# Issuing a kernel's first work ahead of its block, and waiting for its stores behind the block's closing barrier

## The chip, the cores and the metric

The kernel runs on one core of a Trainium2 chip. The metric is the device time of one execution in microseconds. The profile also gives the span, from the first to the last instruction that it recorded in this program. Here the metric is longer than the span (129.3 against 127.56 us in the profiled run of the kernel before). A semaphore is a counter by which the engines and the loads and stores tell each other that something is done; a load or store lands when its last packet is counted on its semaphore. A run is called slow when it lies over 1.5% above the fastest of its kernel.

## The reference

Six cross layers are applied to 4096 rows of 416 numbers in bfloat16:

```python
def reference(x0, ws, bs):          # (4096, 416), (6, 416, 416), (6, 416)
    x = x0
    for l in range(ws.shape[0]):
        x = x0 * (x @ ws[l] + bs[l]) + x
    return x
```

## The kernel before

The rows are worked through in four stages of 1024, the features as three blocks of 128 and a tail of 32. TensorE multiplies, VectorE and ScalarE add the bias and multiply by x0, GpSimd does the tail. All the code of the engines stands in one block: each engine jumps into its own body at the block's start (my reading of the program; the traces have no record of this jump) and out of it at its end (the trace before records SyncE's branch alone, at 127.177 us), and the end of the block is a barrier of all five (in the same trace GpSimd collects the others at 127.379 and releases them at 127.456). The change touches only the two edges of the block.

```python
    with ExitStack() as es:
        block = es.enter_context(nc.Block())
        # ... buffers, semaphores ...

        @block.sync
        def _(sp):
            # ...
            sp.dma_start(bsa_sb[1:L + 1, :], bs[:, :]).then_inc(s_bs, 16)
            sp.dma_start(xin_sb[:, 0:2, :], x0_v[:, 0:2, :]).then_inc(s_xin[0], 16)
            sp.dma_start(xin_sb[:, 4:6, :], x0_v[:, 4:6, :]).then_inc(s_xin[2], 16)
            sp.dma_start_transpose(x0T_sb[:, :, 768:SB], x0[768:SB, 0:DF]).then_inc(s_x0T[0], 16)
            # ... weights, stages ...
            store(sp, 0, 2, 0)
            store(sp, 4, 2, 2)
            sp.wait_ge(s_out, 16 * (NS + 3))

        @block.tensor
        def _(pe):
            # ...
            fill(10)          # 40 matmuls of constants, to keep TensorE busy
            bias_sums()       # waits for the biases, the memsets and GpSimd's setup
            fill(1)
            # ... transposes of the first rows; then stages, each layer ~84 matmuls
            # before the first layer's third block of features:
                                pe.wait_ge(s_xin[2], 16)
                                pe.wait_ge(s_xtl0, 16)
                                tail_inputs()

        @block.scalar
        def _(act):
            act.dma_start(xin_sb[:, 2:4, :], x0_v[:, 2:4, :]).then_inc(s_xin[1], 16)
            act.dma_start(w_sb[:, 0, :, :], wmain(0)).then_inc(s_w[0], 16)
            act.dma_start(xtl_sb[:, :, :], x0_v[:, 6:JS, DF:D]).then_inc(s_xtl0, 16)
            # ...
            act.wait_ge(s_o, JS - 2)
            act.dma_start(out_w[:, (j0 + 6) // 2, :, :], o_sb[:, j0 + 6:j0 + JS, :]).then_inc(s_out, 16)
```

## Time and profile before

| | before |
|---|---|
| time, first three runs | 129.58 us median (129.36 to 129.74) |
| span of the profiled run (its time) | 127.56 us (129.3 us) |
| dense part of TensorE | 6.77 to 124.57 us |
| landing of the last store | 127.160 us |

The stretches of the kernel before, cut at the start and the end of the dense part, one row each: length, then busy microseconds and instructions of TensorE, its weight loads, VectorE, ScalarE and GpSimd, then the granted TensorE clock, the DMA share and GB/s.

```profile
0.00:6.77 6.77, 5.58 (x96) 3.64 (x97) 2.12 (x7) 1.94 (x3) 4.34 (x13) 1.00 0.82 202
6.77:124.57 117.80, 117.78 (x2242) 58.45 (x2242) 97.18 (x146) 65.63 (x143) 19.77 (x31) 1.00 0.48 98
124.57:127.60 3.03, 0.00 (x0) 0.00 (x0) 0.59 (x1) 0.00 (x0) 0.00 (x0) 0.99 0.51 191
```

In the middle row TensorE is busy for all but 0.02 us. Nothing that the change touches lies there. The first row is an opening under loads (DMA share 0.82), the last row has one VectorE instruction in it and otherwise stores and barriers.

### The profile page before, as it was taken

What the parts mean: (1) busy time and instruction counts of PE and PEld (TensorE: products, weight loads), DVE (VectorE), ACT (ScalarE), POOL (GpSimd) and SP (SyncE); (2) the same over time, 40 slices, a digit from 0 to 9 for tenths busy, and PEclk for the clock granted to TensorE, in tenths of its full rate; (3) what the DMA queues carried; (4) which work ended last, traced back from release to release, by engine and by line L of the source; (5) the groups of instructions that cost most, each with busy time, mean ns of one, the idle gap of its engine ahead of it and who ended that gap; (6) DMA issues with size and microseconds to landing.
All of it is one profiled execution on the core that took longest, in us unless ns stands there. A gap on an engine that the chain in (4) does not pass through costs nothing.

```text
span 127.6 us, 5176 instructions
## 1 busy us (share of the span) xinstructions
PE 123.4 (97%) x2338; PEld 62.1 (49%) x2338; DVE 99.9 (78%) x154; ACT 67.6 (53%) x146; POOL 24.1 (19%) x44
## 2 busy tenths in 40 slices
PE   7999999999999999999999999999999999999990
PEld 5554545445444445445445445445445444444660
DVE  2349779779779779779789788798797797797872
ACT  0637357377726456475735554574753573576630
POOL 7512202202102013012022023022022022020460
PEclk9999999999999999999999999999999999999999
DMA  3973399400009899710008679950007910620015
GB/s 100 292 182 100 91 214 212 128 0 0 5 8 143 127 117 231 244 47 5 0 5 152 124 121 242 347 161 0 5 0 48 208 22 0 208 64 5 0 63 204
DMA packets 32576, 13.48 MB, mean 106 GB/s; under 512 B 24870, under 2 KB 32556, under 8 KB 32556
## 3 DMA queue, kind: packets, MB, share of 16 engines
q1 hardware_dynamic: 31036, 12.12, 45.7%
q10 hardware_dynamic: 1328, 0.99, 2.5%
q8 instruction: 18, 0.29, 1.0%
q0 software_dynamic: 192, 0.06, 0.2%
q14 instruction: 2, 0.02, 0.1%
HBM read 3.86 MB, written 3.41 MB: 57 GB/s over the span
## 4 chain that ended last, share of the span: by engine, by line
PE 92%; DMA 4%; ACTq 1%; DVE 0%; issue 0%
PE ps L243 78%; PE ps L374 10%; DMA xtl_sb<-in_x_dram 4%; PE ps L422 3%; PE ps L430 1%; DVE o_sb L518 0%; ACTq L526 0%; PE ps L454 0%; ACTq L525 0%; PE ps L390 0%; PE ps L460 0%
## 5 line engine op out<-in xcount | busy, mean ns | idle before, releaser
L505 DVE SCALAR_TENSOR_TENSOR xT_sb<-ps,cb_sb,x0T_sb 128x512 bf16<-128x512 f32 x120 | 81.0, 744 | 16.5 <-PE ps L374 16.4
L243 PE MATMUL ps<-xT_sb,w_sb 128*32 128x512 bf16 (+1 forms) x1596 | 84.2, 364 | 0.0
L243 PEld LDWEIGHTS ps<-xT_sb,w_sb 128*32 128x32 bf16 x1596 | 40.9, 97 | 37.2 <-issue 4.0
L537 ACT ACTIVATE xt_sb<-xt_sb 32x256 bf16<-32x256 bf16 x76 | 31.5, 414 | 15.8 <-POOL xt_sb L220 15.1
L566 ACT ACTIVATE t_sb<-ps,cb_sb 64x256 f32<-64x256 f32 x46 | 21.6, 469 | 31.2 <-PE ps L243 30.9
L220 POOL TENSOR_TENSOR xt_sb<-t_sb,x0t_sb 128x256 bf16<-128x256 f32 x20 | 13.5, 674 | 81.5 <-ACT t_sb L566 81.5
L243 PE MATMUL ps<-x0T_sb,w_sb 128*32 128x512 bf16 (+1 forms) x336 | 18.5, 364 | 0.2 <-DVE x0T_sb L480 0.2
L505 DVE SCALAR_TENSOR_TENSOR xo_sb<-ps,cb_sb,x0T_sb 128x512 bf16<-128x512 f32 x18 | 12.1, 743 | 2.5 <-PE ps L374 2.5
L243 PEld LDWEIGHTS ps<-x0T_sb,w_sb 128*32 128x32 bf16 x336 | 8.6, 97 | 7.7 <-issue 0.8
L374 PE MATMUL ps<-xt_sb,wt_sb 32*128 32x512 bf16 x76 | 11.5, 379 | 0.0
L585 ACT ACTIVATE x0t_sb<-x_sb 32x512 bf16<-32x512 bf16 x12 | 7.5, 626 | 0.3
L390 PE MATMUL ps<-xt_sb,wt_sb 32*128 32x512 bf16 x38 | 7.4, 385 | 0.0
L374 PE MATMUL ps<-xt_sb,wc_sb 32*128 32x256 bf16 x76 | 7.3, 268 | 0.0
L374 PEld LDWEIGHTS ps<-xt_sb,wt_sb 32*128 32x128 bf16 x76 | 2.2, 92 | 8.1 <-DVE xT_sb L505 8.1
L422 PE MATMUL ps<-w_sb,xT_sb 128*128 128x416 bf16 x24 | 5.4, 340 | 0.0
L374 PEld LDWEIGHTS ps<-xt_sb,wc_sb 32*128 32x128 bf16 x76 | 3.8, 93 | 2.2
L220 POOL TENSOR_TENSOR xot_sb<-t_sb,x0t_sb 128x256 bf16<-128x256 f32 x3 | 2.0, 676 | 12.6 <-ACT t_sb L566 12.6
L518 DVE SCALAR_TENSOR_TENSOR o_sb<-ps,x0n_sb 128x416 bf16<-128x416 f32 x6 | 3.3, 586 | 1.1 <-PE ps L460 1.0
L541 ACT ACTIVATE xo_sb<-ps,cq_sb 128x512 bf16<-128x512 f32 x5 | 3.3, 686 | 1.1 <-PE ps L374 1.1
L243 PE MATMUL ps<-const-bfloat16-1.0 128*32 128x256 bf16 x44 | 2.7, 415 | 0.8 <-PEq L612 0.8
L532 ACT ACT_TABLE_LOAD x1 | 1.3, 1283 | 3.6 <-issue 3.6
L422 PEld LDWEIGHTS ps<-w_sb,xT_sb 128*128 128x128 bf16 x24 | 2.0, 98 | 1.4 <-DVE xT_sb L505 0.4
(46 smaller groups left out, 36.8 us busy)
## 6 DMA issues: line engine op xcount, KB each, us to landing
out_dram<-o_sb SPq DMA_DIRECT2D x3, 832.0 KB, 5.7
w_sb<-in_ws_dram SPq DMA_DIRECT2D x5, 312.0 KB, 4.5
x0n_sb<-in_x_dram SPq DMA_DIRECT2D x1, 832.0 KB, 5.5
xin_sb<-in_x_dram SPq DMA_DIRECT2D x2, 208.0 KB, 3.7
out_dram<-o_sb SPq DMA_DIRECT2D x2, 208.0 KB, 2.0
out_dram<-o_sb ACTq DMA_DIRECT2D x2, 208.0 KB, 2.0
w_sb<-in_ws_dram ACTq DMA_DIRECT2D x1, 312.0 KB, 3.7
xin_sb<-in_x_dram ACTq DMA_DIRECT2D x1, 208.0 KB, 2.7
```

The lines of the kernel that those rows point to most:

```text
L220: pool.tensor_tensor(out=dst, in0=t32_sb[:, n % 2, :], in1=x0t_sb[:, s, 0:G], op=ALU.mult).then_inc(s_xt, 1)
L243: return pe.matmul(dst, lhsT=lhsT, rhs=rhs, start=start, stop=True, skip_group_check=True, tile_position=(0, 32 * q),)
L374: return pe.matmul(dst, lhsT=lhsT, rhs=srct[lane(g), cols], start=l == 0 and start, stop=True, skip_group_check=True, tile_position=(32 * ...
L390: pe.matmul(ps[:, NC * h + 2, :], lhsT=wt_sb[lane(g), l, 0:128], rhs=srct[lane(g), :].rearrange("p (b r) -> p b r", b=2)[:, ::-1, :], star ...
L422: pe.matmul(ps[:, NAT_BANKS[t], 0:D], lhsT=xT_sb[:, (L - 1) % 2, k, rows], rhs=w_sb[:, L - 1, k, :], start=t < 4 and k == 0, stop=True, sk ...
L505: dve.scalar_tensor_tensor(out=dst, in0=ps[:, NC * half + c, :], scalar=cb_sb[:, c, l:l + 1], in1=x0T_sb[:, c, o:o + H], op0=ALU.add, op1= ...
L518: dve.scalar_tensor_tensor(out=o_sb[:, j0 + t, :], in0=ps[:, NAT_BANKS[t], 0:D], scalar=1.0, in1=x0n_sb[:, t, :], op0=ALU.add, op1=ALU.mul ...
L532: act.activation(out=x0T_sb[:, 1, h * 256:(h + 1) * 256], in_=psT[:, IN_BANKS[h][1], 0:256], func=ACTF.Copy).then_inc(s_inA, 1)
L537: ins = act.activation(out=buf[lane(g), G:2 * G], in_=buf[lane(g ^ 1), 0:G], func=ACTF.Copy)
L541: act.activation(out=xo_sb[:, NS - 1, c, half * H:(half + 1) * H], in_=ps[:, NC * half + c, :], func=ACTF.Identity, bias=cq_sb[:, c:c + 1] ...
L566: ins = act.activation(out=t32_sb[HALVES[h], n % 2, :], in_=tail(h), func=ACTF.Identity, bias=cb_sb[HALVES[h], NC, l:l + 1],)
L585: ins = act.activation(out=x0t_sb[lane(g), s + 1, :].rearrange("p (b n) -> p b n", b=2), in_=src[:, ::-1, :] if g % 2 else src, func=ACTF. ...
```

## The change

The intent was to take the jump into the block off the path of the first loads, and the closing barrier off the path of the last store. The diff, cut to its core:

```diff
     with ExitStack() as es:
-        block = es.enter_context(nc.Block())
 # ... buffers, semaphores ...
+        for q in range(4 * 10):
+            nc.tensor.matmul(
+                ps[lane(q % 4), 7, 0:256], lhsT=CONST[:, 0:32], rhs=CONST, start=True, stop=True,
+                skip_group_check=True, tile_position=(0, 32 * (q % 4)),
+            )
+        nc.sync.dma_start(bsa_sb[1:L + 1, :], bs[:, :]).then_inc(s_bs, 16)
+        nc.sync.dma_start(xin_sb[:, 0:2, :], x0_v[:, 0:2, :]).then_inc(s_xin[0], 16)
+        nc.sync.dma_start(xin_sb[:, 4:6, :], x0_v[:, 4:6, :]).then_inc(s_xin[2], 16)
+        nc.scalar.dma_start(xin_sb[:, 2:4, :], x0_v[:, 2:4, :]).then_inc(s_xin[1], 16)
+        nc.scalar.dma_start(w_sb[:, 0, :, :], wmain(0)).then_inc(s_w[0], 16)
+        nc.scalar.dma_start(xtl_sb[:, :, :], x0_v[:, 6:JS, DF:D]).then_inc(s_xtl0, 16)
+        nc.gpsimd.memset(ones_sb[:, :], 1.0).then_inc(s_ones, 1)
+        nc.vector.memset(wc_sb[:, :, :], 0.0).then_inc(s_zero, 1)
+        nc.vector.memset(bsa_sb[0:1, :], 1.0).then_inc(s_zero, 1)
+
+        es2 = ExitStack()
+        block = es2.enter_context(nc.Block())
 # ... the same lines leave the bodies of the engines ...
             store(sp, 4, 2, 2)
-            sp.wait_ge(s_out, 16 * (NS + 3))
 # ... end of the last body ...
+        es2.close()
+        nc.sync.wait_ge(s_out, 16 * (NS + 3))
```

More of the change, by code (lines that the diff above doesn't have):

```diff
@@ L111, in tail @@
             return ps[HALVES[h], 6 + h, 0:G]
+        CONST = nc.const_aps.tensor_like(1.0, ones_sb[:, :])
         j0 = (NS - 1) * JS
@@ L138, in load_rows @@
                 ).then_inc(s_x0T[s], 16)
-            sp.dma_start(bsa_sb[1:L + 1, :], bs[:, :]).then_inc(s_bs, 16)
-            sp.dma_start(xin_sb[:, 0:2, :], x0_v[:, 0:2, :]).then_inc(s_xin[0], 16)
-            sp.dma_start(xin_sb[:, 4:6, :], x0_v[:, 4:6, :]).then_inc(s_xin[2], 16)
             sp.dma_start_transpose(x0T_sb[:, :, 768:SB], x0[768:SB, 0:DF]).then_inc(s_x0T[0], 16)
@@ L176, in _ @@
             store(sp, 4, 2, 2)
-            sp.wait_ge(s_out, 16 * (NS + 3))
         @block.gpsimd
         def _(pool):
-            pool.memset(ones_sb[:, :], 1.0).then_inc(s_ones, 1)
             def load_wc(i, g):
@@ L246, in tile_mm @@
                 )
-            const = nc.const_aps.tensor_like(1.0, ones_sb[:, :])
             def fill(n):
@@ L252, in fill @@
                     for q in range(4):
-                        tile_mm(ps[lane(q), 7, 0:256], const[:, 0:32], const, q, True)
+                        tile_mm(ps[lane(q), 7, 0:256], CONST[:, 0:32], CONST, q, True)
             def tail_inputs():
@@ L283, in bias_sums @@
                 ins.then_inc(s_cbp, 1)
-            fill(10)
             bias_sums()
@@ L470, in _ @@
         def _(dve):
-            dve.memset(wc_sb[:, :, :], 0.0).then_inc(s_zero, 1)
-            dve.memset(bsa_sb[0:1, :], 1.0).then_inc(s_zero, 1)
             dve.wait_ge(s_cbp, 1)
@@ L524, in _ @@
         def _(act):
-            act.dma_start(xin_sb[:, 2:4, :], x0_v[:, 2:4, :]).then_inc(s_xin[1], 16)
-            act.dma_start(w_sb[:, 0, :, :], wmain(0)).then_inc(s_w[0], 16)
-            act.dma_start(xtl_sb[:, :, :], x0_v[:, 6:JS, DF:D]).then_inc(s_xtl0, 16)
             for g in (1, 3):
```

## The prediction

Two names in it, and in the expectations further on, stand for one thing in the traces: the serpentine, or the runtime's barrier, is the row of nine raises of semaphore 2 behind the kernel, from 127.799 to 128.345 us in the trace before. A hop is the time from one raise to the next. The records show the raises and their times, not what makes them.

> **What bounds the kernel now.** I read the page's first and fourth parts, then the chain of waits in order of time for the opening, then the sync queue's own waits for the end, and last the trace's raw records of semaphores, drains and branches at both edges, because the change touches nothing else.
>
> The page says that one engine carries the span:
>
> ```profile
> span 127.6 us, 5176 instructions
> ...
> PE 92%; DMA 4%; ACTq 1%; DVE 0%; issue 0%
> ```
>
> The reader is to see that the matrix engine is on the chain for 92% of 127.6 us. None of that work is in the diff: the 40 filler matmuls that move are outside the chain. So the change can only shift the start of the dense part and shorten what follows it.
>
> The chain of waits for the first 14 us (start, duration, what) shows what the dense part starts from:
>
> ```profile
> 0.74 0.07 issue
> 0.80 0.44 ACTq L525
> 1.24 0.03 issue
> 1.27 0.49 ACTq L526
> 1.76 0.03 issue
> 1.79 4.85 DMA xtl_sb<-in_x_dram
> 6.64 0.14 issue
> 6.77 1.40 PE ps L243 x52
> ```
>
> The start hangs on ScalarE's third load, which is queued behind its first two. It is issued at 1.79 and lands at 6.64; from 6.77 the matrix engine is busy until 124.57 (111.51 us busy in the 111.51 us from 6.77 to 118.28). So a load issued earlier by x moves everything behind it by about x, if its flight of 4.85 us doesn't change.
>
> The timeline of the opening (start, duration, engine) shows that all engines begin together:
>
> ```profile
> 0.79 0.31 POOL L181 MEMSET ones_sb<- 128x256 bf16 x1 [0.29 <-POOLq L612]
> 0.80 0.39 SPq L140 DMA_DIRECT2D bsa_sb<-in_bs_dram  x1
> 0.80 0.44 ACTq L525 DMA_DIRECT2D xin_sb<-in_x_dram  x1
> ```
>
> L612 is the construction of the program object, which writes four constants and holds a barrier of all engines. In the raw records GpSimd writes the constants from 0.31 to 0.50, drains until 0.55, collects the others at 0.60, and releases them at 0.67; their own records of the release end at 0.732 (SyncE), 0.737 (ScalarE), 0.747 (VectorE) and 0.778 (TensorE).[...]
>
> The sync queue's own waits at the end:
>
> ```profile
> engine line waited for: us in total, times, longest us
> SPq L122 <- DVE o_sb L518: 13.8, 1, 13.8
> SPq L33 <- DMA out_dram<-o_sb: 2.4, 1, 2.4
> SPq L120 <- POOL o_sb L236: 1.0, 1, 1.0
> SPq L33 <- PEq L33: 0.2, 1, 0.2
> ```
>
> L33 is the block itself. SyncE waits 2.4 us there for the stores, and only then, 0.2 us more, for the closing barrier. The raw records give the order: ScalarE issues the last store at 125.22; its landing is counted at 127.160; SyncE's branch out of the block, which carries the wait, runs at 127.177; SyncE drains at 127.340; GpSimd collects at 127.379 and releases at 127.456; the last engine's release ends at 127.560, where the span ends. ScalarE's drain, the last of the other four, was done at 125.79. So four engines stood at the barrier for about 1.4 us, and 0.38 us of barrier then comes after the landing.
>
> [...]from the end of the release to the first instruction SyncE takes 66 ns and ScalarE 65 ns, where two issues of ScalarE that follow each other are 29 and 30 ns apart.[...]
>
> [...]semaphore 2 is raised nine times from -0.371 to 0.000, nine times from 127.799 to 128.345, and nine times from 129.132 to 129.489 (0.357 us). The middle one, right after the kernel, took 0.546 us because two hops were long (0.225 and 0.097, where the others are 0.02 to 0.05).
>
> [...]The last store took 127.160 - 125.22 = 1.94 us for 208 KB; the change doesn't shorten it.
>
> **The change part by part.**
>
> 1. The jump leaves the path of the loads. ScalarE's first load should follow the release at the 30 ns of its other gaps in place of 65: 0.035 us earlier. Its second and third load move with it. SyncE's loads gain about the same. Its jump now stands after the third load; the transpose that follows (2.22) stays where it was, as do ScalarE's two small weight loads (2.33). On the path: -0.03 to -0.05 us, so the dense part starts at about 6.73.
>
> 2. The fillers, memsets and GpSimd's constants. The fillers are there to be done by 3.08, when the bias row has landed (2.20) and the setup is ready; the gap before them isn't on the chain. VectorE's memset could start 0.2 us earlier (0.965 against a release at 0.747); its second one ends at 1.85, and the matmuls that need it run at 3.08. Worth 0.
>
> 3. The wait behind the closing barrier. The barrier is passed near 126.0 (ScalarE's drain at 125.79 plus the 0.22 us from SyncE's drain to the last release, 127.340 to 127.560), which is over a microsecond before the stores land. Then the landing is followed by one wait of 17 ns, the usual length of such a record. The end of the span is 127.160 + 0.017 + 0.017 = 127.19 in place of 127.56: -0.37 us.
>
> 4. What follows the span. The measured time is longer than the span by 129.3 - 127.56 = 1.74 us in the profiled run[...]. When SyncE arrives alone and late, the others are ready. If its place is at the head of the serpentine, the whole of it then runs at the clean 0.36 us in place of 0.546: a further -0.18; if it sits in the middle, fewer hops are left, -0.3; if the long hop was SyncE's own, nothing. I count -0.10, an estimate.
>
> Sum: 0.04 + 0.37 + 0.10 = 0.51 us. 129.58 - 0.51 = 129.07, rounded to 129.1. The span should come to about 127.56 - 0.04 - 0.37 = 127.15.
>
> **The rivals.**
>
> *Only the span gains, or less.* The runtime's barrier might cost the same after a late SyncE as after five engines together, or the program may end with a hidden jump after the wait. For it: the first raise of semaphore 2 came 0.28 us after SyncE's release, so there is unrecorded work of its own. Against: that work is there in both kernels. The time would be 129.2.
>
> *The loads' flight takes the gain back.* From about 2.5 us the transfers run at 340 to 378 GB/s, and the third ScalarE load is behind 520 KB of its own queue and beside SyncE's. Moving all issues together leaves the order alone[...]. If the whole opening gain is lost, 129.1 still; if the flight grows by 0.3 us, 129.4. For it: flights of loads in this opening range from 2.7 to 5.4 us. Against: each queue's sequence is unchanged.
>
> *The jump comes back elsewhere.* It could land in front of the transpose or the small weight loads and make the tail inputs late. These land at 7.64 (transpose) and 7.76 (weights) against uses at about 8.65 and 8.10: 0.3 us and more to spare[...]. Worth 0.
>
> *A real loss.* [...]a barrier that the block adds on entry once something stands ahead of it. The kernel before has the program's constants ahead of the same block and shows no second barrier, so I give it very little[...].
>
> **How the range and the chances follow.** 2% of 129.58 is 2.6 us; the edges that the change can touch are the 0.06 us jump, the 0.38 us barrier and a serpentine of 0.55 us, under 1 us together. A gain over 2% is therefore out of reach, and a loss over 2% would need a fault that nothing shows. The three runs before spread over 129.36 to 129.74, so a median of a few runs is good to about 0.1 to 0.15. Gains from 0.15 to 0.85 us cover the rivals and that noise: 128.75 to 129.4.
>
> **What would show each step right or wrong.** Step 1: ScalarE's first load at 0.76 to 0.77 in place of 0.80, the third load's landing at about 6.60, and the first dense matmul at about 6.73. Step 2: the bias matmuls still near 3.05. Step 3: in the sync queue's waits the wait for the stores comes last and stands at a line of its own, no wait for another engine follows it, and the span ends under 0.05 us after the last landing. Step 4: the serpentine after the kernel ended 128.345 - 127.160 = 1.19 us after the landing; with steps 3 and 4 right it ends some 1.19 - 0.37 - 0.10 = 0.7 us after it, with step 4 at nothing 0.8. It would be wrong if the store's own flight grew, or if the dense part started later than 6.77 because a load lost its place.

## The result

| | before | changed |
|---|---|---|
| median, same rounds (6 runs each) | 129.46 us (129.04 to 129.74) | 128.69 us (128.43 to 130.87) |
| ratio of the fast runs, 95% interval | | 0.994 (0.9915 to 0.9965) |
| profiled run: time, span | 129.3, 127.56 us | 128.78, 127.55 us |

A ratio is the mean time of one kernel's fast runs over that of the other's of the same rounds, so it is not quite the ratio of the medians quoted. The run of 130.87 us is slow and is left out of it. The change is worth 0.77 us by the medians; without the slow run the changed kernel's median is 128.59 us, 0.87 us less than before. This is within 2%, as forecast, but outside the stated range: 128.69 is below 128.75, and 0.77 us is half as much again as the 0.51 us of the prediction's sum.

The puzzle is in the last row: the two profiled runs differ by 0.52 us in time and by 0.01 us in span. The page of the changed kernel begins and is carried as before:

```profile
span 127.5 us, 5176 instructions
...
PE 92%; DMA 4%; ACTq 1%; DVE 0%; issue 0%
```

The opening of the changed kernel in the chain of waits (start, duration, what; L137 to L139 are now ScalarE's three loads):

```profile
0.74 0.07 issue
0.80 0.43 ACTq L137
1.23 0.03 issue
1.26 0.49 ACTq L138
1.76 0.03 issue
1.78 5.13 DMA xtl_sb<-in_x_dram
6.92 0.14 issue
7.05 1.40 PE ps L255 x52
```

The reader is to see two things. The first load is still issued at 0.80, and the third at 1.78 in place of 1.79: nothing was gained by standing ahead of the jump. And in this execution the third load flew 5.13 us in place of 4.85, so the dense part started 0.28 us later. The later profiles of the same loads, below, speak for chance.

The stretches of the changed kernel, cut in the same way:

```profile
0.00:7.05 7.05, 5.72 (x96) 3.71 (x97) 2.15 (x7) 1.94 (x3) 4.33 (x13) 1.00 0.82 192
7.05:124.91 117.86, 117.85 (x2242) 58.42 (x2242) 97.18 (x146) 65.62 (x143) 19.72 (x31) 1.00 0.48 98
124.91:127.60 2.69, 0.00 (x1) 0.00 (x0) 0.59 (x1) 0.00 (x0) 0.00 (x0) 1.00 0.58 216
```

The dense part has the same instructions and the same length within 0.06 us; what was lost ahead of it (0.28) is nearly what is saved behind it. The sync queue's own waits at the end of the changed kernel:

```profile
SPq L121 <- DVE o_sb L525: 13.8, 1, 13.8
SPq L605 <- DMA out_dram<-o_sb: 1.2, 1, 1.2
SPq L119 <- POOL o_sb L248: 1.0, 1, 1.0
SPq L604 <- PEq L604: 1.0, 1, 1.0
```

The order has turned round: L604, the end of the block, is waited for during 1.0 us, and then L605, the wait for the stores, 1.2 us more, with nothing behind it. The raw records, counted from the landing of the last store, show what the span cannot (semaphore 2 is raised nine times in a row behind the kernel; times in us):

```
                          before   changed
span ends                  0.400    0.033
raises of semaphore 2:  1  0.639   -0.921
                        2  0.674   -0.887
                        3  0.899   -0.661
                        4  0.944   -0.618
                        5  0.967    0.150
                        6  1.064    0.195
                        7  1.103    0.233
                        8  1.139    0.267
                        9  1.185    0.315
last raise of all          2.329    1.460
```

From the landing to the last raise of all, the changed kernel needs 0.869 us less: 0.367 lie in the span, 0.503 behind it, up to the ninth raise, and what follows the ninth raise takes 1.144 and 1.145 us. In these two runs the measured times go with the last raise of all: counted from the start of the span it comes at 129.489 and 128.974 us, and the times are 129.3 and 128.78 us, 0.19 us less in both. The last matmul ended 0.355 us later (124.913 in place of 124.558); 0.869 - 0.355 = 0.514 us is what remains of the gain between these two runs, whose times differ by 0.52 us. In the changed kernel four raises are made while the stores fly, and only five are left.

### The profile page after: what moved, and what is told of

It is laid out like the page before. It is cut to its first block, busy times and chain, and to the rows that moved or that the text cites.

```text
span 127.5 us, 5176 instructions
## 1 busy us (share of the span) xinstructions
PE 123.6 (97%) x2338; PEld 62.1 (49%) x2338; DVE 99.9 (78%) x154; ACT 67.6 (53%) x146; POOL 24.1 (19%) x44
## 4 chain that ended last, share of the span: by engine, by line
PE 92%; DMA 4%; ACTq 1%; DVE 0%; issue 0%
PE ps L255 78%; PE ps L383 10%; DMA xtl_sb<-in_x_dram 4%; PE ps L431 3%; PE ps L439 1%; DVE o_sb L525 0%; ACTq L138 0%; PE ps L463 0%; ACTq L137 0%; PE ps L399 0%; PE ps L469 0%
```

## The experiments

The theory after this comparison was: the opening is worth nothing, and the end is worth 0.87 us, of which 0.50 come from the other four engines getting through their own unrecorded work and their turns in the row of nine raises while SyncE waits alone. The rivals were that the opening contributes, and that it is enough to have the closing barrier out of the way. Every kernel gave a correct result.

### The end alone

```diff
-        block = es.enter_context(nc.Block())
+        es2 = ExitStack()
+        block = es2.enter_context(nc.Block())
 # ...
-            sp.wait_ge(s_out, 16 * (NS + 3))
 # ...
+        es2.close()
+        nc.sync.wait_ge(s_out, 16 * (NS + 3))
```

> The kernel before with one edit: the wait for the stores stands behind the block's closing barrier; loads, memsets and fillers stay in the block. Theory (all of the gain is at the end: 0.37 us of closing barrier and 0.50 us of the runtime's own barrier): about 0.8 us faster than before, the same as the changed kernel within 0.15 us; raises of semaphore 2 after the kernel: four before the landing, five after it, the last some 0.3 us after the landing. Rival (a part of the gain comes from the opening): 0.3 us slower than the changed kernel or more.

Measured: 128.49 us median against 129.64 of before in these rounds. The ratio, 0.991 (0.9866 to 0.9954), flatters it, since the runs of before that were counted as fast include one of 131.08. From the landing the span ended after 0.034, the ninth raise came after 0.315 and the last raise of all after 1.460 us, within a nanosecond of the changed kernel. Against the changed kernel in the same rounds (128.85) it is 0.36 us faster by the medians, more than the 0.15 us that was expected; the means of the time less the span are 1.26 us in both, so this difference lies in the span and not at the end. The end alone is the whole of the gain.

### The opening alone

```diff
             store(sp, 4, 2, 2)
+            sp.wait_ge(s_out, 16 * (NS + 3))
 # ...
         es2.close()
-        nc.sync.wait_ge(s_out, 16 * (NS + 3))
```

> The changed kernel with one edit undone: the wait for the stores is back inside the block. Theory (the jump costs nothing where it stood): the same as before within 0.15 us, ScalarE's and SyncE's first loads at 0.80 us as in both kernels, runtime barrier ending about 1.18 us after the landing. Rival (the early issue is worth the recorded prediction's 0.04 us or more): first loads at 0.76 us; a gain over 0.2 us would speak for it, one of 0.04 us is under what the times can show and only the records could.

Measured: 129.63 us median against 129.64; ratio 0.9987 (0.9939 to 1.0036). First loads at 0.798 and 0.802 us, and 2.321 us from the landing to the last raise of all (before: 2.329). The opening is worth nothing that shows. The records also say why: the gap after the barrier's release is there with and without a jump in it (SyncE 66 ns in both kernels), and where the jump stands now, behind the third load, the gap is the one that was there without it (SyncE 45 in place of 44 ns, ScalarE 30 in place of 29).

This execution shows a chance that runs through all times. TensorE's stretch before the dense part, in the timeline of this kernel:

```profile
5.13 2.50 PE L256 MATMUL ps<-x0T_sb,w_sb 128*32 128x512 bf16 x24
```

These 24 matmuls took 1.48 us in the kernel before and in the changed one. The records of the granted clock have full speed from 4.65 us in the former, 4.91 in the latter, and from 7.24 here. Over all profiles that have this record, that moment lay between 4.05 and 9.55 us; three executions of one and the same kernel, the changed one, had 4.91, 4.57 and 5.20. So I take it for a chance of the execution, which no run proves. It can move a single time by more than the edits do (these 24 matmuls alone by 1.02 us here), and so I read small effects from the records, counted from the landing.

### All engines wait for the stores

```diff
         es2.close()
-        nc.sync.wait_ge(s_out, 16 * (NS + 3))
+        for eng in (nc.sync, nc.scalar, nc.vector, nc.gpsimd, nc.tensor):
+            eng.wait_ge(s_out, 16 * (NS + 3))
```

> The changed kernel, but behind the closing barrier all five engines wait for the stores, not SyncE alone. Theory (0.50 us come from the other four engines doing their unrecorded work and their turns in the runtime's barrier while the stores fly): the span still ends within 0.1 us of the landing, no raise of semaphore 2 before the landing, the last one about 0.85 us after it instead of 0.3; 0.5 us slower than the changed kernel, 0.3 us faster than before. Rival (it is enough that the closing barrier is out of the way): equal to the changed kernel.

Measured: 129.54 us median against 129.64 (ratio 0.9994, 0.9946 to 1.0041), and against 128.85 of the changed kernel in the same rounds. The sync queue's own waits of this kernel:

```profile
SPq L121 <- DVE o_sb L525: 13.8, 1, 13.8
SPq L606 <- DMA out_dram<-o_sb: 1.2, 1, 1.2
SPq L119 <- POOL o_sb L248: 1.0, 1, 1.0
SPq L604 <- PEq L604: 1.0, 1, 1.0
```

They are the same as in the changed kernel, and the span, too, ends close to the landing (0.079 us after it). But the nine raises come from 0.275 to 0.883 us after the landing, and the last of all at 2.027 in place of 1.460: 0.567 us lost, 0.52 of it behind the span. The times show this and more: time less span was 1.96 to 2.06 us in the six runs of this kernel, and 1.24 to 1.29 in those of the changed kernel beside it, so 0.76 us by the means. So taking the closing barrier out of the way is not enough. By the raises, a gain of 2.329 - 2.027 = 0.30 us against before should be left; the medians show 0.10, less than was expected, and the interval of the ratio holds both.

In nine of the fourteen profiles the time, counted from the start of the span, is 0.18 to 0.19 us short of the last raise of all; in this kernel it is 0.06 us beyond it. So about 0.25 us of its loss stand in no raise. The same 0.25 us are found in two kernels below, `wait_gpsimd` (the wait on GpSimd) and `xtl_pool` (the first try at a faster opening), and these three are the kernels whose traces record one instruction more on GpSimd (59 in place of 58). In the two other exceptions, the wait on ScalarE and the third try, ScalarE has one more (182 in place of 181), and the time is 0.09 and 0.05 us short of the last raise. What this time is spent on, no record shows.

### The changed kernel again, twice

> The changed kernel as it is, for the same chip and rounds. Theory: 0.7 to 0.85 us faster than before. If its third ScalarE load lands near 6.6 us this time and not at 6.92, the later landing in its first profile was a chance of that execution; if near 6.9 again, the change delays it.

> The changed kernel as it is, as the control of the same rounds: 0.7 to 0.9 us faster than before, last raise of the runtime's barrier 0.31 us after the landing as in its two other profiles.

Measured: 128.85 against 129.64 us (ratio 0.9933, 0.9877 to 0.9988; one run of 129.95 is in it), and, in the last rounds, 128.45 against 129.58 (0.993, 0.9902 to 0.9958). Gains by the medians: 0.79 and 1.13 us; the second was more than expected. The ninth raise came 0.314 and 0.316 us after the landing. The third ScalarE load landed at 6.84 and 6.59 us. In the nine profiles in which the same loads are issued ahead of the block it landed between 6.01 and 6.92 us (mean 6.54), in the two with the old opening at 6.64 and 6.48. So the late landing of the first profile reads as chance, not as an effect of the change.

### The wait on each of the other engines

```diff
         es2.close()
-        nc.sync.wait_ge(s_out, 16 * (NS + 3))
+        nc.scalar.wait_ge(s_out, 16 * (NS + 3))      # also: vector, gpsimd, tensor
```

In the changed kernel four raises came before the landing and five after it. The theory reads from this that SyncE's turn is the fifth of nine, and that the other four engines come ahead of it, one raise each; ahead of these runs that was an estimate.

> The changed kernel with the wait for the stores behind the barrier on ScalarE in place of SyncE. Theory[...]: ScalarE stands earlier in the row, so fewer than four raises come before the landing, and the last one 0.4 to 0.9 us after it in place of 0.31. Rival (any one engine that waits alone does as well): four raises before, last one 0.28 to 0.35 us after.

> The wait on VectorE in place of SyncE. Theory: fewer than four raises of semaphore 2 before the landing, the last one 0.4 to 0.9 us after it. Rival: as with SyncE, 0.28 to 0.35 us.

> The wait on GpSimd in place of SyncE. Theory: fewer than four raises of semaphore 2 before the landing, the last one 0.4 to 0.9 us after it. Rival: as with SyncE, 0.28 to 0.35 us.

> The wait on TensorE in place of SyncE. Theory: fewer than four raises of semaphore 2 before the landing, the last one 0.4 to 0.9 us after it; over the four engines of this call the counts of raises before the landing are 0, 1, 2 and 3, one each. Rival: as with SyncE, 0.28 to 0.35 us.

Each ran once, so the state is unknown and the times (128.74, 128.91, 131.19, 130.65 us, and 131.46 for the kernel before) say little: in the last two the full clock was granted only from 9.55 and 9.44 us. Counted from the landing, the records (one profile for each engine but SyncE) say a lot:

```
who waits   raises before   end of its   its own raise   ninth    last raise
            the landing     wait record  (after that)    raise    of all
TensorE     0               0.079        0.275 (0.196)   0.633    1.779
ScalarE     1               0.038        0.152 (0.114)   0.476    1.622
GpSimd      2               0.041        0.597 (0.556)   0.882    2.031
VectorE     3               0.049        0.203 (0.154)   0.445    1.589
SyncE       4               0.033        0.150 (0.117)   0.315    1.460
```

The counts 0, 1, 2, 3 and 4 give the order of the first five raises: TensorE, ScalarE, GpSimd, VectorE, SyncE. That the other four go back through the row is my estimate, from nine raises for five engines; it was not shown. An engine that came late here paid its own work after its last recorded instruction (the number in brackets) and then the rest of the row. GpSimd has by far the most work of its own, 0.556 us. The theory's numbers held for all four (one count each, 0.4 to 0.9 us), the rival's (0.28 to 0.35 for any engine) for none. By the ninth raise SyncE is the best place of the five: the least but one of own work, and the shortest rest of the row.

### Three tries at a faster opening

The dense part waited for the small load of the tail columns, third in ScalarE's queue. Three versions issue it elsewhere.

```diff
-        nc.scalar.dma_start(xtl_sb[:, :, :], x0_v[:, 6:JS, DF:D]).then_inc(s_xtl0, 16)
+        nc.gpsimd.dma_start(xtl_sb[:, :, :], x0_v[:, 6:JS, DF:D]).then_inc(s_xtl0, 16)   # ahead of the memset
```

> A try at a version that beats both: the changed kernel, with the small load of the tail columns, on which the dense part waited (landing 6.64 in the profile before, 6.92 in the one after), issued first by GpSimd at about 0.8 us in place of third by ScalarE at 1.79. If its late landing is a matter of its place in the queue, it lands before 5 us; the dense part then starts when the third input block has landed (5.5 to 6.5) and the first 24 dense matmuls are through (6.6), so at 6.6 in place of 6.6 to 7.05: 0 to 0.4 us faster than the changed kernel, 0.8 to 1.2 faster than before. Rival: GpSimd's setup of the identity comes 0.8 us later and holds the first transposes (3.62), which takes the gain back; equal to the changed kernel or slower.

Measured: 129.46 against 129.56 us (ratio 1.0015, 0.9982 to 1.0048), so as slow as before, where the changed kernel gains 0.8 us or so in its rounds (it was not run in these). GpSimd issued the load only at 1.32 us and took 0.99 us over it; it landed at 5.96, not before 5 us as was expected. The dense part began at 6.54, as hoped, but had to wait again, which the waits of this kernel show:

```profile
PE ps L383 <- DMA wc_sb<-in_ws_dram: 0.5, 1, 0.5
```

GpSimd's own weight loads (the corner of the weights, tail features by tail features) had been pushed back with everything else in its queue; the chain ended their flight at 8.65 us. Not all of the loss is in the opening: time less span is 1.44 to 1.52 us here, 0.25 us more than in the changed kernel, with the same raises; these are the 0.25 us noted above.

The second version puts the small load first in ScalarE's queue:

```diff
+        nc.scalar.dma_start(xtl_sb[:, :, :], x0_v[:, 6:JS, DF:D]).then_inc(s_xtl0, 16)
         nc.scalar.dma_start(xin_sb[:, 2:4, :], x0_v[:, 2:4, :]).then_inc(s_xin[1], 16)
         nc.scalar.dma_start(w_sb[:, 0, :, :], wmain(0)).then_inc(s_w[0], 16)
-        nc.scalar.dma_start(xtl_sb[:, :, :], x0_v[:, 6:JS, DF:D]).then_inc(s_xtl0, 16)
```

> The same aim with ScalarE: the small load goes first in its queue, the two large ones 0.5 us later. The first transposes would wait for the second input block (landing 4.0 in place of 3.5) and the dense part for the first weights (5.5 in place of 5.0), so the first 24 matmuls end at about 7.1: no gain, 0 to 0.4 us slower than the changed kernel. If it is faster, the small load alone held the start.

Measured: 130.56 us against the same 129.56 (ratio 1.0082, 1.0049 to 1.0116; without a slow run its median is 130.28), worse than expected. The small load landed at 2.60, but the weights, issued 0.5 us later, landed at 6.46 in place of about 5.0, and they carry the chain. The 24 matmuls behind them also took longer, 2.23 us in place of 1.48; whether the edit or chance did that is open.

```profile
1.79 4.67 DMA w_sb<-in_ws_dram
6.46 0.04 issue
6.51 2.50 PE ps L255 x40
```

The third version is the GpSimd one with GpSimd's other two weight loads given to ScalarE:

```diff
-        nc.scalar.dma_start(xtl_sb[:, :, :], x0_v[:, 6:JS, DF:D]).then_inc(s_xtl0, 16)
+        nc.gpsimd.dma_start(xtl_sb[:, :, :], x0_v[:, 6:JS, DF:D]).then_inc(s_xtl0, 16)
 # gpsimd's body
-            for g in (0, 2):
-                load_wt(pool, g, 0, 1, s_wtp)
 # scalar's body, behind its own two
+            for g in (0, 2):
+                load_wt(act, g, 0, 1, s_wtp)
```

> The GpSimd version once more, with GpSimd's two other small weight loads moved to ScalarE's queue, so that the loads that held it last time (the corner weights, landing 8.65) are issued about 1 us earlier and land near 7.7. If the start of the dense part is now all that counts: dense part from 6.5 to 6.6 and no later wait, 0 to 0.4 us faster than the changed kernel in the same rounds. Rival: ScalarE's four small weight loads end later (the last issued near 3.4, landing near 8.0 against a use near 7.8), and the wait comes back there; equal to the changed kernel or up to 0.3 us slower.

Measured: 128.88 against 129.58 us (ratio 0.9954, 0.9931 to 0.9977), and against 128.45 of the changed kernel in the same rounds, so 0.43 us slower than that, more than even the rival allowed. The new wait is gone, as expected, but nothing was gained: GpSimd's setup of the identity, later by the load's issue, holds the transposes from 3.62 to 3.83, and the 24 matmuls run to 6.88 in this profile, where the full clock came at 5.88. The start is then TensorE's own, and the load that the chain had named was only the last of several limits that lie close together. Of the 0.43 us, 0.10 lie behind the span (1.35 us on average in place of 1.25). None of the three beats the changed kernel.

## Why the prediction was wrong, point by point

**What bounds the kernel, and the 2%.** Right. The dense part kept its 117.8 us in both profiles, and all of the difference lies at the edges.

**Step 1, "the jump leaves the path of the loads", -0.04 us.** Failed. It took the whole gap of 65 ns behind the barrier's release for the jump. The changed kernel has no jump there and the same gap; the first loads came at 0.800 and 0.804 in place of 0.798 and 0.802. Where the jump stands now it adds a nanosecond (45 in place of 44 ns on SyncE, 30 in place of 29 on ScalarE). The step's measured size in the records is 0. The times of the opening alone (0.9987, with an interval of half a per cent to each side) agree, but could not have shown 0.04 us.

**Step 2, fillers, memsets and setup, 0.** Right in size. The bias matmuls ran at 3.09 as before. VectorE's memset did not start 0.2 us earlier either, as the step thought it could: 0.967 in place of 0.965.

**Step 3, the wait behind the closing barrier, -0.37 us.** Right in mechanism and size: the span ends 0.033 us after the landing in place of 0.400. The wait for the stores comes last, and no other engine is waited for behind it.

**Step 4, what follows the span, -0.10 us as an estimate.** This is the term that was mis-sized: 0.503 us by the two profiles. With it the sum is 0.87 us, just over the 0.85 us of gain that the range allowed; with 0.10 it would have been 0.47, well inside. On which side of the edge the result fell was in part luck of the base: the range starts from the 129.58 us of three runs, where the six runs of before had 129.46, and the gain by the medians, 0.77 us, lies inside 0.15 to 0.85.

The step weighed places in the row (0.18 for the head, 0.3 for the middle, 0 for an unlucky one) and settled on a number between them. Its reading of the row had two faults. It took two hops for long ones, but the hop of 0.097 is normal (0.098 in the last row of the same trace, 129.132 to 129.489); only the one of 0.225 was a delay, where 0.038 is usual. And it saw that delay as part of the row, when it is the tail of something longer: GpSimd's raise, the third, came 0.586 us after GpSimd's last recorded instruction. Before, that work could only begin when the closing barrier had released GpSimd, 0.313 us after the landing. The path was 0.313 + 0.586 + the six hops left, 0.286 = 1.185 us. In the changed kernel GpSimd does it while the stores fly, and the path is SyncE's: 0.033 + 0.117 + four hops of 0.165 in all = 0.315 us. "If it sits in the middle" was the right case for SyncE, whose raise is the fifth of the nine, but GpSimd's work was not in the sum at all. The unrecorded work that the prediction did notice, 0.28 us, it gave to SyncE; it is TensorE's, whose own raise is the first and came 0.239 us after its release. When the work is put back behind the landing (all engines wait) 0.567 us come back; when GpSimd alone waits, 0.571.

**Taken together.** 0 + 0.37 + 0.50 = 0.87 us, in place of 0.51. Both parts of the end were right in direction; the larger one fell short by 0.40 us because GpSimd's own work was missing from it. Over the runs timed with the experiments, without the slow ones, the changed kernel's mean is 128.71 us (12 runs) and that of before 129.56 (28 runs): 0.85. Of this, 0.35 is in the span (127.46 against 127.81) and 0.50 in the time behind it (1.25 against 1.75), which hardly varies: 1.22 to 1.29 us in those 12 runs of the changed kernel, 1.70 to 1.79 in all 33 of before. Chip and rounds differ among these runs, so the figure for the part behind the span is the firmer of the two.

**The rivals.** "Only the span gains, or less" fell: the part behind the span was the larger. "The loads' flight takes the gain back" happened in the first profile (0.28 us) as a chance of the execution, not as an effect of the change. "The jump comes back elsewhere" and "a real loss" did not occur.

**What stays open.** What GpSimd does in its 0.56 us, what the 0.25 us of measured time are that three kernels have behind their raises, and why the full clock is granted at such different moments, no run here settles.

## What to carry to other kernels

Let a kernel's last wait, the one for its stores, stand behind the last barrier and on one engine alone, so that all the others finish their leaving work while the stores fly: in the two profiles here this took 0.869 us off the time from the landing to the last raise of all. Of the five, SyncE was the cheapest to come late here (0.315 us from the landing to the ninth raise) and GpSimd the dearest (0.882 us). When the measured time and the span don't agree, follow the semaphore records past the span's end: here more than half of the gain (0.503 of 0.869 us) lay where the page shows nothing. Before counting a gap as the cost of the instruction that stands in it, look for the same gap where that instruction is absent (here 66 ns on SyncE, with the jump and without).
